# Which weights come first in a decode layer: w_1 and the MLP's features moved ahead of w_q

## The chip, the cores and the metric

The kernel runs on one core of one Trainium2 chip. The metric is device time in microseconds (us), the median of several executions. A profile of one execution says where the time of that execution lies. The core has five engines that run side by side and wait for each other by semaphores: TensorE (PE, matrix products), VectorE (DVE), ScalarE (ACT), GpSimd (POOL) and SyncE (SP). Here SP does nothing but issue transfers, one after the other, so a transfer that has to wait holds back all the transfers behind it. ACT issues a few small transfers on a queue of its own.

## What is computed

One token goes through two branches, which a gate mixes:

```python
g = sigmoid((x * gate_w).sum(-1))                       # one number
q = x @ wq                                              # 576 -> 32 heads of 128
k, v = the last 4096 of 32768 positions of the caches   # 16 heads, each for two query heads
a = softmax(q k^T / sqrt(128)) v  @ wo                  # attention branch
b = gelu(x @ w1 + b1) @ w2 + b2                         # MLP branch, 576 -> 4608 -> 576
out = g * a + (1 - g) * b
```

Everything is bfloat16 in memory. With one token each weight and each cached key is used once, so the work is to read 53.62 MB: four key tiles and four value tiles of 4096 KB each, w_q and w_o with 4608 KB each, w_1 with 5184 KB and w_2 with as much.

## The kernel before

**Tiles and buffers.** The 16 key/value heads are done four at a time, t = 0 to 3. Key tile k_t[t] and value tile v_t[t] hold four heads of the window. All eight, and w_2's two halves after them, go through one pool of three buffers (kv_pool, L80); a new tile is loaded when the buffer's last reader is done. w_q, w_1 and w_o share one buffer (w_pool, L81). The order of the program on each engine is that of the text (manual_schedule, L90).

**Order of the transfers on SP.** w_q, k_0, k_1, b_1, the gate's weights, k_2, v_0, k_3, w_1, v_1, v_2, v_3, w_o, w_2 in five pieces, and the output. By the three buffers, v_0 takes k_0's place, k_3 takes k_1's, v_1 takes k_2's, v_2 takes v_0's, v_3 takes k_3's, and w_2's halves take v_1's and v_2's. Each of these is issued when the last reader of the old tile is done: for keys the DVE transposes, for values the matmuls of `values`. w_1 needs the buffer of w_q, and w_o that of w_1, which `w1_mul` reads last. Besides, the transfers take their completion semaphores in turn from a set of eight, so that the ninth shares one with the first and waits until that one has landed. In this program the first is w_q's, and the ninth is the first piece of the gate's weights (L151).

**Start.** x comes as one row (L137), is copied to an order by partitions (L171, ACT), spread over the partitions by nine matmuls with a one-element operand (L377) and masked by four DVE instructions into x2 (L387). Then 36 matmuls make q (L392), it is turned and written with zeros between into qz, the operand of the scores (L404 to L428).

**Attention.** Key tile t has four quarters, h = 4t to 4t+3. DVE transposes each (`transposes(h)`, L243) into one of four buffers kT, and eight matmuls of 512 columns make its scores (`scores(h)`, L265). For h below 12 a loop pass is scores(h), one step of the softmax of the tile before, transposes(h+4); for the last four it is transposes(h), scores(h), one step. `softmax(t)` is four steps: row_max (DVE, L284 and L289), turn_max (a PE transpose, L295, then DVE L296 and L299), spread (PE L306, DVE L307, the exponential on ACT L310) and turn (DVE, L316). `values(t)` is 32 matmuls (L335), and `heads_out(t)` takes their result (L353 to L367). `norm` makes the divisors (L530 to L542).

**Gate and MLP.** `gate_rows` (L510) stands after the second key tile's transposes, `gate` (L517 to L522) after the third tile's scores. `w1_mul`, 72 matmuls with w_1 (L449), stands behind the last scores; `gelu` (L468 to L497), which makes the features gt, stands behind `norm` and before `values(1)`.

**End.** The partial sums `part` take w_o's product for one half of the rows, then w_2's first half, then the rest of w_o (L664). They are copied (L672, L673) and added to y_ps, which takes b_2 times 1 - g first (L652, eight small matmuls, listed under L647) and the second half of w_2 row by row as its pieces land (L675 to L688). y goes out by L694.

Of the kernel before, what the change touches and what calls it, by code (L numbers as in the profile page):

```python
# [8 lines left out]
FP32 = mybir.dt.float32  # L9
# [7 lines left out]
def kernel(  # L17
# [15 lines left out]
    nc = tc.nc  # L33
# [78 lines left out]
    def load_k(m):  # L112
        return load_kv(A_k_cache, m, "k_t")

    def load_v(m):
        return load_kv(A_v_cache, m, "v_t")
# [3 lines left out]
    def load_flat(src, name):  # L120
        t = w_pool.tile([P, WMAX], BF16, name=name, tag="w")
        nc.sync.dma_start(out=t[:, 0 : src.shape[1]], in_=src)
        return t
# [7 lines left out]
    nc.gpsimd.memset(b2_r[:], 0.0)  # L131
    b2_f = const.tile([1, D], FP32, name="b2_f")

    for h in (slice(0, D // 2), slice(D // 2, D)):
        nc.scalar.dma_start(out=b2_r[:, h], in_=B_b2.rearrange("(o n) -> o n", o=1)[:, h])

    nc.scalar.dma_start(out=x_row[:], in_=A_x.rearrange("a b n -> (a b) n"))  # L137

    wq_t = load_flat(wq_flat, "wq_t")
    k_tiles[0] = load_k(0)  # L140

    k_tiles[1] = load_k(1)
    b1_r = const.tile([P, 2, FB], BF16, name="b1_r")
    nc.gpsimd.memset(b1_r[:], 0.0)
    for o in range(2):
        nc.sync.dma_start(
            out=b1_r[o : o + 32 * (NQ - 1) + 1 : 32],
            in_=B_b1.rearrange("(o t k n) -> o t k n", o=2, t=NQ, k=2)[o],
        )
    for h in (slice(0, D // 2), slice(D // 2, D)):  # L150
        nc.sync.dma_start(out=gw_row[:, h], in_=gate_w.rearrange("(o n) -> o n", o=1)[:, h])  # L151
    k_tiles[2] = load_k(2)


    ident = const.tile([P, P], BF16, name="ident")
    make_identity(nc, ident[:])
# [10 lines left out]
        out=row_f[:], in_=ident_f[:, 0 : 32 * (NQ - 1) + 1 : 32], axis=AX.X, op=ALU.add  # L167
    )

    x_d = small.tile([1, P, NM], BF16, name="x_d", tag="ms")  # L170
    nc.scalar.copy(  # L171
        out=x_d[:].rearrange("o (k e) m -> o k e m", e=2),
        in_=x_row[:].rearrange("o (k e m) -> o k e m", e=1, m=NM).to_broadcast(
            [1, P // 2, 2, NM]
        ),
    )
    nc.scalar.copy(out=b2_f[:], in_=b2_r[:])
    one = const.tile([1, 1], BF16, name="one")
    nc.gpsimd.memset(one[:], 1.0)
    par = const.tile([P, 2], FP32, name="par")  # L180
    for o in range(2):
        nc.vector.tensor_reduce(
# [57 lines left out]
    def transposes(h):  # L240
        kT[h] = kT_pool.tile([P, NCH * ND], FP32, name="kT", tag="kT")
        lo = (h % UT) * NCH * Dh
        nc.vector.transpose(  # L243
            out=kT[h][:],
            in_=k_tiles[h // UT][:].rearrange("p c d -> p (c d)")[:, lo : lo + NCH * Dh].bitcast(
                FP32
            ),
        )
# [124 lines left out]


    x_ps = ps_m.tile([P, NM], FP32, name="x_ps", tag="m")
    for m in range(NM):
        nc.tensor.matmul(  # L377
            x_ps[:, m : m + 1], lhsT=x_d[0:1, :, m], rhs=one[:], start=True, stop=True
        )
    ev, od = par[:, 0:1], par[:, 1:2]  # L380
    for dst, src, s in (
        (x2[:, 0::2, 0], x_ps[:, 0:5], ev),
# [2 lines left out]
        (x2[:, 1::2, 1], x_ps[:, 0:4], ev),  # L385
    ):
        nc.vector.tensor_scalar(out=dst, in0=src, scalar1=s, scalar2=None, op0=ALU.mult)  # L387

    q_ps = ps_a.tile([P, 2, 512], FP32, name="q_ps", tag="a")
    for b in range(NM * NQ):  # L390
        m, t = b // NQ, b % NQ
        nc.tensor.matmul(  # L392
            q_ps[32 * t : 32 * (t + 1), 0, 0:QC],
            lhsT=x2[:, m, :],
            rhs=wq_t[:, b * QC : (b + 1) * QC],
            start=(m == 0),
            stop=(m == NM - 1),
        )
    NI = QC // Dh
    qT = q_ps[:, 1, 0 : NI * NBP * 2 * NT].rearrange("p (i b n) -> p i b n", i=NI, b=NBP)  # L400
    q_r = small.tile([P, NI, NBP, NA, PI], BF16, name="q_r", tag="big")
    for i in range(NI):
        copy = nc.scalar.copy if i % 2 else nc.vector.tensor_copy
        copy(  # L404
            out=q_r[:, i].rearrange("p (b o) a u -> p b o a u", b=2)[:, :, :, 0, :],
            in_=q_ps[:, 0, i * Dh : (i + 1) * Dh].rearrange("p (b u o) -> p b o u", b=2, o=2),
        )
    for i in range(NI):
        copy = nc.scalar.copy if i % 2 else nc.vector.tensor_copy
        copy(  # L410
            out=q_r[:, i, :, 1:NA, :],
            in_=q_r[:, i, :, 0:1, :].to_broadcast([P, NBP, NA - 1, PI]),
        )
    for i in range(NI):
        for bp in range(NBP):
            nc.tensor.matmul(
                qT[:, i, bp, :],
                lhsT=q_r[:, i, bp].rearrange("p a u -> p (a u)"),
                rhs=sel[:].rearrange("p l b -> p (l b)"),
                start=True,  # L420
                stop=True,
            )


    for a in range(NA):
        rows = slice(PI * a, PI * (a + 1))
        lo = QX + PI * a
        nc.vector.tensor_copy(  # L428
            out=qz[rows, lo : lo + NR * QW].rearrange("p (b t w) -> p b t w", b=NBP, w=QW)[
                :, :, :, 0:R  # L430
            ].rearrange("p b t (l i) -> p b t l i", l=2),
            in_=qT[rows].rearrange("p i b (l t) -> p b t l i", l=2),
        )


    for h in range(UT):
        transposes(h)
    v_tiles[0] = load_v(0)

    U = F // 2  # L440
    h_box = []
# [66 lines left out]
    def gate_rows():  # L508
        junk = small.tile([1, D], BF16, name="junk", tag="big")
        nc.vector.tensor_tensor_reduce(  # L510
            out=junk[:], in0=x_row[:], in1=gw_row[:], scale=1.0, scalar=0.0,
            op0=ALU.mult, op1=ALU.add, accum_out=s0[:],
        )

    def gate():
        g_ps = ps_m.tile([P, 1], FP32, name="g_ps", tag="m")
        nc.tensor.matmul(g_ps[:], lhsT=ones_ff[0:1, :], rhs=s0[:], start=True, stop=True)  # L517
        ge = const.tile([P, 1], FP32, name="ge")
        nc.scalar.activation(out=ge[:], in_=g_ps[:], func=ACT.Exp, scale=-1.0)
        nc.vector.tensor_scalar(out=ge[:], in0=ge[:], scalar1=1.0, scalar2=None, op0=ALU.add)  # L520
        nc.vector.reciprocal(out=g_t[:], in_=ge[:])
        nc.vector.tensor_scalar(  # L522
            out=omg[:], in0=g_t[:], scalar1=-1.0, scalar2=1.0, op0=ALU.mult, op1=ALU.add
        )
# [28 lines left out]

    for h in range(UT):
        scores(h)
        transposes(h + UT)
    k_tiles[3] = load_k(3)
    w1_t = load_flat(w1_flat, "w1_t")  # L560
    chain = softmax(0)
    for h in range(UT, 2 * UT):
        scores(h)
# [1 line left out]
        transposes(h + UT)  # L565
    v_tiles[1] = load_v(1)
    chain = softmax(1)
    gate_rows()
    for h in range(2 * UT, 3 * UT):
        scores(h)  # L570
        chain.pop(0)()
        if h == 3 * UT - 2:
            values(0)
            v_tiles[2] = load_v(2)
    gate()
    chain = softmax(2)
    for h in range(3 * UT, 4 * UT):
        transposes(h)
        scores(h)
        chain.pop(0)()  # L580
    v_tiles[3] = load_v(3)
    w1_mul(w1_t)
    wo_t = w_pool.tile([P, WMAX], BF16, name="wo_t", tag="w")
    nc.sync.dma_start(out=wo_t[:, 0 : OJ * D], in_=wo_view[:, 0, :])
    row_max, turn_max, spread, turn = softmax(3)
    take, turn_out = heads_out(0)
    take_h, turn_h, act = gelu()
    row_max()
    turn_max()
    spread()  # L590
# [1 line left out]
    turn()  # L592
    turn_out()
    norm()
    take_h()
    turn_h()
    act()
    sums_start()
    values(1)
    take, turn_out = heads_out(1)  # L600
# [44 lines left out]
    def row_matmul(col, row, start, stop):  # L645
        for t, q in enumerate(parts):
            nc.tensor.matmul(  # L647
                y_ps[32 * t : 32 * t + 1, 0 : q.stop - q.start], lhsT=col, rhs=row[:, q],
                start=start, stop=stop,
            )  # L650

    row_matmul(omg[0:1, :], b2_f, True, False)  # L652

    part = part_box[0]
    late = [[(ow[:, i, 0:1], wo_t, i) for i in range(j, j + NQ)] for j in range(0, OJ, NQ)]
    blocks, late = late[: OJ // (2 * NQ)], late[OJ // (2 * NQ) :]
# [1 line left out]
        blocks.append([(gt[:, i, 0:1], w2_t[0], i) for i in range(j, min(j + NQ, RJ))])  # L658
    blocks += late
    last = {t: max(n for n, four in enumerate(blocks) if t < len(four)) for t in range(NQ)}  # L660
    for n, four in enumerate(blocks):
        for k in range(2):
            for t, (col, w, i) in enumerate(four):
                nc.tensor.matmul(  # L664
                    part[32 * t : 32 * t + 1, k, 0:DB],
                    lhsT=col,
                    rhs=w[:, i * D + k * DB : i * D + (k + 1) * DB],
                    start=(n == 0),
                    stop=(n == last[t]),
                )  # L670
    part_s = [const.tile([P, DB], FP32, name=f"part_{k}") for k in range(2)]
# [2 lines left out]

    for j in range(RJ):  # L675
        row_matmul(
            gt[:, j, NG - 1 : NG], w2_t[NG - 1][:, j * D : (j + 1) * D], False, j == RJ - 1
        )
        if j == JA - 1:
            for t, q in enumerate(parts):  # L680
                for k in range(2):
                    lo, hi = max(q.start, k * DB), min(q.stop, (k + 1) * DB)
                    if lo < hi:
                        nc.tensor.matmul(
                            y_ps[32 * t : 32 * t + 1, lo - q.start : hi - q.start],
                            lhsT=row_f[:], rhs=part_s[k][:, lo - k * DB : hi - k * DB],
                            start=False, stop=False,
                        )  # L688
# [36 lines left out]
```

## Time and profile before

| | |
|---|---|
| median of 3 executions | 133.68 us (133.24 to 133.75) |
| the profiled execution, its own time | 133.42 us |
| its span, first to last instruction | 131.6 us |
| mean granted clock of TensorE | 0.78 |
| busy: PE, DVE, ACT, POOL | 72.6, 73.5, 10.7, 3.9 us |
| DMA: bytes, share of 16 engines in the SP queue's packets | 53.70 MB, 95.2% |
| chain that ended last: DMA, DVE, PE | 40%, 35%, 17% of the span |

The span is 1.82 us shorter than the execution's own time. In the fences below, a line of the timeline has the start in us, the busy us, the engine, the source line, the operation and its count; in brackets stand the idle time ahead of it and what ended it. A line of the waits has who waited for whom, the sum in us, how often, and the longest. A line of the chain that ended last has the start, the us and what it was. Lines of the stretches (windows) give the stretch and its length, then the busy us of PE, weight loads, DVE, ACT and POOL, and as the last three numbers PE's granted clock, the DMA engines' busy share and GB/s.

### The profile page before, as it was taken

The numbers are of one execution on the slowest core, as the hardware profiler recorded it, in microseconds if no ns is written. First come the engines' busy times: TensorE is split into PE (matmuls) and PEld (weight loads), VectorE is DVE, ScalarE is ACT, GpSimd is POOL, SyncE is SP. The second block draws the span as 40 slices with busy tenths as digits, with TensorE's granted clock in tenths as the row PEclk, the third lists the DMA queues.
The fourth block names the chain that finished last, engine by engine and source line by source line (L and its number), as shares of the span: only waits on it lengthen the run. The fifth ranks groups of instructions, "written<-read, shape, count | busy, mean of one in ns | idle before, by whom it ended". The sixth has DMA issues, their size and how long they took to land.

```text
span 131.6 us, 1446 instructions
## 1 busy us (share of the span) xinstructions
PE 72.6 (55%) x602; PEld 31.4 (24%) x602; DVE 73.5 (56%) x113; ACT 10.7 (8%) x20; POOL 3.9 (3%) x11
## 2 busy tenths in 40 slices
PE   0000293099892299919919665398275655460781
PEld 0000232034330134303313212135130321130451
DVE  2900103999799999981379434647778347300011
ACT  2100504000000003000300000300300000000011
POOL 8300000000000000000000000000000000000000
PEclk9999999658999757986985559559955599655589
DMA  6898999999999899899999999999998989899960
GB/s 179 370 527 359 478 408 398 468 448 390 440 463 428 378 478 458 378 431 515 403 403 403 486 383 448 468 408 398 478 448 373 483 370 527 363 416 425 413 226 0
DMA packets 2337, 53.70 MB, mean 408 GB/s; under 512 B 270, under 2 KB 540, under 8 KB 668
## 3 DMA queue, kind: packets, MB, share of 16 engines
q1 hardware_dynamic: 2326, 53.62, 95.2%
q8 instruction: 4, 0.07, 0.2%
q14 instruction: 1, 0.01, 0.0%
q10 hardware_dynamic: 6, 0.00, 0.0%
HBM read 53.62 MB, written 0.00 MB: 407 GB/s over the span
## 4 chain that ended last, share of the span: by engine, by line
DMA 40%; DVE 35%; PE 17%; issue 4%; SPq 1%; ACT 0%; DVEq 0%
DMA k_t<-in_A_k_cache_dram 24%; DVE kT L243 19%; DMA w_t<-in_B_w_dram 16%; PE s_ps L265 11%; PE acc L335 4%; DVE ms L284 4%; DVE mx L289 3%; DVE a_s L357 2%; DVE hT L474 1%; DVE ez L316 1%; PE mb L306 1%; PE mT L295 1%; DVE h_r L468 1%; DVE m L296 1%; DVE m_all L299 0%
## 5 line engine op out<-in xcount | busy, mean ns | idle before, releaser
L265 PE MATMUL s_ps<-kT,qz 128*128 128x512 bf16 x128 | 40.6, 479 | 14.0 <-DVE kT L243 14.0
L243 DVE STREAM_TRANSPOSE kT<-k_t 128x2048 f32<-128x2048 f32 x16 | 36.1, 2285 | 1.0 <-DMA k_t<-in_A_k_cache_dram 0.9
L265 PEld LDWEIGHTS <-qz 128*128 128x128 bf16 x128 | 14.5, 115 | 36.5 <-issue 27.1
L335 PE MATMUL acc<-v_t,ez 128*32 128x512 bf16 x128 | 11.0, 488 | 0.0
L310 ACT ACTIVATE pr<-ms,nb 128x1024 bf16<-128x1024 f32 x4 | 4.6, 1148 | 64.7 <-DVE nb L307 64.7
L377 PE MATMUL x_ps<-one,x_d 1*128 1x1 bf16 x9 | 0.7, 195 | 14.8 <-ACT x_d L171 14.8
L672 DVE COPY part<-part 128x288 f32<-128x288 f32 x1 | 0.5, 457 | 12.8 <-PE part L664 12.8
L284 DVE TENSOR_TENSOR ms<-s_ps,off 128x1024 f32<-128x1024 f32 x4 | 4.8, 1210 | 2.3 <-PE s_ps L265 2.2
L365 PE MATMUL o_ps<-a_s,m_r 128*32 128x128 f32 x8 | 1.9, 319 | 7.7 <-DVE a_s L357 7.7
L295 PE MATMUL mT<-ident_f,mx 128*1 128x128 f32 x4 | 1.4, 358 | 8.3 <-DVE mx L289 8.3
L387 DVE TENSOR_SCALAR x<-x_ps,par 128x5 bf16<-128x5 f32 (+1 forms) x4 | 0.6, 229 | 9.2 <-PE x_ps L377 9.2
L316 DVE STREAM_TRANSPOSE ez<-pr 128x1024 bf16<-128x1024 bf16 x4 | 4.9, 1221 | 1.4 <-ACT pr L310 1.4
L664 PE MATMUL part<-wo_t,ow 128*1 128x288 bf16 x64 | 4.4, 427 | 1.7 <-DMA wo_t<-in_A_wo_dram 1.7
L335 PEld LDWEIGHTS <-ez 128*32 128x32 bf16 x128 | 4.2, 117 | 4.4 <-issue 2.9
L289 DVE TENSOR_REDUCE mx<-ms 128x1 f32<-128x1024 f32 x4 | 4.9, 1220 | 0.1
L664 PE MATMUL part<-w_t,gt 128*1 128x288 bf16 x36 | 2.6, 441 | 4.0 <-DMA w_t<-in_B_w_dram 4.0
L357 DVE SCALAR_TENSOR_TENSOR a_s<-acc,m_c,a_s 128x128 f32<-128x128 f32 x12 | 4.2, 351 | 0.4
L392 PE MATMUL q_ps<-wq_t,x 128*32 128x512 bf16 x36 | 4.0, 630 | 0.6 <-DVE x L387 0.6
L377 PEld LDWEIGHTS <-x_d 1*128 1x128 bf16 x9 | 0.6, 152 | 14.8 <-ACT x_d L171 14.8
L307 DVE TENSOR_SCALAR nb<-mb 128x1 f32<-128x1 f32 x4 | 0.6, 145 | 6.2 <-PE mb L306 6.2
L296 DVE TENSOR_REDUCE m<-mT 1x8 f32<-1x128 f32 x4 | 1.1, 268 | 4.7 <-PE mT L295 4.7
L158 DVE CAST ident_f<-ident 128x128 f32<-128x128 bf16 x1 | 1.9, 1900 | 2.3 <-POOL ident masks.py:199 2.3
(86 smaller groups left out, 49.5 us busy)
## 6 DMA issues: line engine op xcount, KB each, us to landing
k_t<-in_A_k_cache_dram SPq DMA_DIRECT2D x4, 4096.0 KB, 22.8
v_t<-in_A_v_cache_dram SPq DMA_DIRECT2D x4, 4096.0 KB
w_t<-in_B_w_dram SPq DMA_DIRECT2D x1, 5184.0 KB, 33.1
wq_t<-in_A_wq_dram SPq DMA_DIRECT2D x1, 4608.0 KB
wo_t<-in_A_wo_dram SPq DMA_DIRECT2D x1, 4608.0 KB
w_t<-in_B_w_dram SPq DMA_DIRECT2D x1, 2592.0 KB
w_t<-in_B_w_dram SPq DMA_DIRECT2D x1, 1872.0 KB
w_t<-in_B_w_dram SPq DMA_DIRECT2D x1, 576.0 KB, 21.4
```

The source lines that it names most:

```text
L243: nc.vector.transpose(out=kT[h][:], in_=k_tiles[h // UT][:].rearrange("p c d -> p (c d)")[:, lo : lo + NCH * Dh].bitcast(FP32),)
L265: nc.tensor.matmul(s_tiles[t][:, k].rearrange("p c i e -> p c (i e)"), lhsT=qz[:, r * QW + lo : r * QW + lo + P], rhs=kT_v[:, k * NCB : (k ...
L284: nc.vector.tensor_tensor(out=ms[:], in0=s_v, in1=off[:].rearrange("p (o e) -> p o e", o=1).to_broadcast([P, NCH * 8, HT]), op=ALU.add,)
L289: nc.vector.tensor_reduce(out=mx[:], in_=ms[:].rearrange("p x e -> p (x e)"), axis=AX.X, op=ALU.max)
L295: nc.tensor.transpose(out=mT[:], in_=mx[:], identity=ident_f[:])
L296: nc.vector.tensor_reduce(out=m8[:], in_=mT[:].rearrange("o (x r) -> o r x", r=R), axis=AX.X, op=ALU.max)
L310: nc.scalar.activation(out=pr[:].rearrange("p c j -> p (c j)"), in_=ms[:].rearrange("p x e -> p (x e)"), func=ACT.Exp, bias=nb[:, 0:1], sc ...
L316: nc.vector.transpose(out=ez[:, t].rearrange("p x c r -> p c x r"), in_=pr[:].rearrange("p c j -> p (c j)"),)
L335: nc.tensor.matmul(acc[t][32 * ct : 32 * ct + BC * R, :, :], lhsT=ez[:, t, x, c : c + BC, :].rearrange("p c r -> p (c r)"), rhs=v_tiles[t] ...
L357: nc.vector.scalar_tensor_tensor(out=a_s[:], in0=acc[t][:, c, :], scalar=m_c[:, c : c + 1], in1=a_s[:], op0=ALU.mult, op1=ALU.add,)
L392: nc.tensor.matmul(q_ps[32 * t : 32 * (t + 1), 0, 0:QC], lhsT=x2[:, m, :], rhs=wq_t[:, b * QC : (b + 1) * QC], start=(m == 0), stop=(m == ...
L664: nc.tensor.matmul(part[32 * t : 32 * t + 1, k, 0:DB], lhsT=col, rhs=w[:, i * D + k * DB : i * D + (k + 1) * DB], start=(n == 0), stop=(n ...
```

## The change

w_1 becomes SP's first transfer and k_0 the second. The making of q (L389 to L433) moves behind the first four transposes, its text unchanged. w_q follows k_0 and takes w_1's buffer, so it waits for `w1_mul`; k_1 and k_2 stand behind it. `w1_mul`, the gate and gelu are done right after x2, ahead of the first transposes and of q. x comes a second time as 64 rows of 9 (x9), and one matmul with a doubled identity (dup) spreads it. The small loads (b_2, x9, b_1, x, gate weights) are all issued by ACT. b_2's product goes into part's first quarter as its first two matmuls, ahead of w_o's, and no longer into y_ps.

As built, the changed kernel issues on SP: w_1; k_0; w_q; k_1; k_2; v_0; k_3; v_1; v_2; v_3; w_o; w_2 in five pieces; the output. The seven small transfers on ACT and w_1's take the eight completion semaphores; k_0 is the ninth, shares w_1's, and its issue waits until w_1 has landed. w_q waits for w_1's last reader (PE); w_o now waits only for w_q's landing and last reader, and all value tiles wait as before.

```diff
+    x9 = const.tile([P // 2, NM], BF16, name="x9")
     for h in (slice(0, D // 2), slice(D // 2, D)):
         nc.scalar.dma_start(out=b2_r[:, h], ...)
...
-    wq_t = load_flat(wq_flat, "wq_t")
-    k_tiles[0] = load_k(0)
-    k_tiles[1] = load_k(1)
...
+    nc.scalar.dma_start(out=x9[:], in_=A_x.rearrange("a b (i m) -> (a b i) m", m=NM))
     for o in range(2):
-        nc.sync.dma_start(
+        nc.scalar.dma_start(
             out=b1_r[o : o + 32 * (NQ - 1) + 1 : 32], ...
+    nc.scalar.dma_start(out=x_row[:], ...)
+    nc.scalar.dma_start(out=gw_row[:], ...)
+    w1_t = load_flat(w1_flat, "w1_t")
+    k_tiles[0] = load_k(0)
...
-    for m in range(NM):
-        nc.tensor.matmul(
-            x_ps[:, m : m + 1], lhsT=x_d[0:1, :, m], rhs=one[:], start=True, stop=True
-        )
+    nc.tensor.matmul(x_ps[:], lhsT=dup[:], rhs=x9[:], start=True, stop=True)
...
+    w1_mul(w1_t)
+    wq_t = load_flat(wq_flat, "wq_t")
+    k_tiles[1] = load_k(1)
+    k_tiles[2] = load_k(2)
+    gate_rows()
+    gate()
+    for f in gelu():
+        f()
+    for h in range(UT):
+        transposes(h)
+    v_tiles[0] = load_v(0)
+    q_ps = ps_a.tile([P, 2, 512], FP32, name="q_ps", tag="a")
...
     for h in range(UT):
         scores(h)
         transposes(h + UT)
     k_tiles[3] = load_k(3)
-    w1_t = load_flat(w1_flat, "w1_t")
...
-    gate_rows()
...
-    gate()
...
-    w1_mul(w1_t)
...
-    take_h()
-    turn_h()
-    act()
...
-    row_matmul(omg[0:1, :], b2_f, True, False)
...
+    for k in range(2):
+        nc.tensor.matmul(
+            part[0:1, k, 0:DB], lhsT=omg[0:1, :], rhs=b2_f[:, k * DB : (k + 1) * DB],
+            start=True, stop=False,
+        )
```

More of the change, by code (lines that the diff above doesn't have):

```diff
@@ L132 @@
     b2_f = const.tile([1, D], FP32, name="b2_f")
+    x9 = const.tile([P // 2, NM], BF16, name="x9")
+    b1_r = const.tile([P, 2, FB], BF16, name="b1_r")
+    nc.gpsimd.memset(b1_r[:], 0.0)
     for h in (slice(0, D // 2), slice(D // 2, D)):
         nc.scalar.dma_start(out=b2_r[:, h], in_=B_b2.rearrange("(o n) -> o n", o=1)[:, h])
-    nc.scalar.dma_start(out=x_row[:], in_=A_x.rearrange("a b n -> (a b) n"))
-    wq_t = load_flat(wq_flat, "wq_t")
-    k_tiles[0] = load_k(0)
-    k_tiles[1] = load_k(1)
-    b1_r = const.tile([P, 2, FB], BF16, name="b1_r")
-    nc.gpsimd.memset(b1_r[:], 0.0)
+    nc.scalar.dma_start(out=x9[:], in_=A_x.rearrange("a b (i m) -> (a b i) m", m=NM))
     for o in range(2):
-        nc.sync.dma_start(
+        nc.scalar.dma_start(
             out=b1_r[o : o + 32 * (NQ - 1) + 1 : 32],
@@ L149 @@
         )
-    for h in (slice(0, D // 2), slice(D // 2, D)):
-        nc.sync.dma_start(out=gw_row[:, h], in_=gate_w.rearrange("(o n) -> o n", o=1)[:, h])
-    k_tiles[2] = load_k(2)
+    nc.scalar.dma_start(out=x_row[:], in_=A_x.rearrange("a b n -> (a b) n"))
+    nc.scalar.dma_start(out=gw_row[:], in_=gate_w.rearrange("(o n) -> o n", o=1))
+    w1_t = load_flat(w1_flat, "w1_t")
+    k_tiles[0] = load_k(0)
     ident = const.tile([P, P], BF16, name="ident")
@@ L168 @@
     )
[L170 to L174, printed above, removed]
-        ),
-    )
-    nc.scalar.copy(out=b2_f[:], in_=b2_r[:])
-    one = const.tile([1, 1], BF16, name="one")
-    nc.gpsimd.memset(one[:], 1.0)
+    nc.scalar.copy(out=b2_f[:], in_=b2_r[:])
+    dup = const.tile([P // 2, P], BF16, name="dup")
+    nc.vector.tensor_copy(
+        out=dup[:].rearrange("k (i e) -> k i e", e=2),
+        in_=ident[0 : P // 2, 0 : P // 2].rearrange("k (i e) -> k i e", e=1).to_broadcast(
+            [P // 2, P // 2, 2]
+        ),
+    )
     par = const.tile([P, 2], FP32, name="par")
@@ L387 @@
         nc.vector.tensor_scalar(out=dst, in0=src, scalar1=s, scalar2=None, op0=ALU.mult)
[L389 to L438, printed above, removed]
     U = F // 2
@@ L550, in sums_start @@
         part_box.append(part)
+    w1_mul(w1_t)
[10 more added lines that the diff above has]
+    q_ps = ps_a.tile([P, 2, 512], FP32, name="q_ps", tag="a")
+    for b in range(NM * NQ):
+        m, t = b // NQ, b % NQ
+        nc.tensor.matmul(
+            q_ps[32 * t : 32 * (t + 1), 0, 0:QC],
+            lhsT=x2[:, m, :],
+            rhs=wq_t[:, b * QC : (b + 1) * QC],
+            start=(m == 0),
+            stop=(m == NM - 1),
+        )
+    NI = QC // Dh
+    qT = q_ps[:, 1, 0 : NI * NBP * 2 * NT].rearrange("p (i b n) -> p i b n", i=NI, b=NBP)
+    q_r = small.tile([P, NI, NBP, NA, PI], BF16, name="q_r", tag="big")
+    for i in range(NI):
+        copy = nc.scalar.copy if i % 2 else nc.vector.tensor_copy
+        copy(
+            out=q_r[:, i].rearrange("p (b o) a u -> p b o a u", b=2)[:, :, :, 0, :],
+            in_=q_ps[:, 0, i * Dh : (i + 1) * Dh].rearrange("p (b u o) -> p b o u", b=2, o=2),
+        )
+    for i in range(NI):
+        copy = nc.scalar.copy if i % 2 else nc.vector.tensor_copy
+        copy(
+            out=q_r[:, i, :, 1:NA, :],
+            in_=q_r[:, i, :, 0:1, :].to_broadcast([P, NBP, NA - 1, PI]),
+        )
+    for i in range(NI):
+        for bp in range(NBP):
+            nc.tensor.matmul(
+                qT[:, i, bp, :],
+                lhsT=q_r[:, i, bp].rearrange("p a u -> p (a u)"),
+                rhs=sel[:].rearrange("p l b -> p (l b)"),
+                start=True,
+                stop=True,
+            )
+    for a in range(NA):
+        rows = slice(PI * a, PI * (a + 1))
+        lo = QX + PI * a
+        nc.vector.tensor_copy(
+            out=qz[rows, lo : lo + NR * QW].rearrange("p (b t w) -> p b t w", b=NBP, w=QW)[
+                :, :, :, 0:R
+            ].rearrange("p b t (l i) -> p b t l i", l=2),
+            in_=qT[rows].rearrange("p i b (l t) -> p b t l i", l=2),
+        )
     for h in range(UT):
@@ L586 @@
     take, turn_out = heads_out(0)
-    take_h, turn_h, act = gelu()
     row_max()
@@ L660 @@
     last = {t: max(n for n, four in enumerate(blocks) if t < len(four)) for t in range(NQ)}
+    for k in range(2):
+        nc.tensor.matmul(
+            part[0:1, k, 0:DB], lhsT=omg[0:1, :], rhs=b2_f[:, k * DB : (k + 1) * DB],
+            start=True, stop=False,
+        )
     for n, four in enumerate(blocks):
@@ L667 @@
                     rhs=w[:, i * D + k * DB : i * D + (k + 1) * DB],
-                    start=(n == 0),
+                    start=(n == 0 and t > 0),
                     stop=(n == last[t]),
@@ L676 @@
         row_matmul(
-            gt[:, j, NG - 1 : NG], w2_t[NG - 1][:, j * D : (j + 1) * D], False, j == RJ - 1
+            gt[:, j, NG - 1 : NG], w2_t[NG - 1][:, j * D : (j + 1) * D], j == 0, j == RJ - 1
         )
```

## The prediction, made before the changed kernel ran

> **What bounds the kernel now.** I read the page's DMA row first, then the stretches, SP's waits, the chain that ended last and the timelines.
>
> The DMA row by slices, and the stretches between five landings that the trace shows (k_1, w_1, w_o, w_2's first half, the last piece):
>
> ```profile
> DMA  6898999999999899899999999999998989899960
> ```
> ```profile
> 1.00:33.60 32.60, 12.82 (x85) 5.68 (x86) 15.56 (x31) 4.36 (x7) 3.46 (x7) 0.90 0.99 419
> 33.60:76.40 42.80, 29.80 (x128) 11.40 (x126) 33.86 (x29) 2.65 (x5) 0.00 (x0) 0.78 1.00 429
> 76.40:116.40 40.00, 21.77 (x212) 9.49 (x211) 23.03 (x50) 2.71 (x5) 0.00 (x0) 0.71 1.00 432
> ```
>
> The DMA share is 0.99, 1.00, 1.00: the transfers never run dry, while no compute engine is full. The end, in the chain, is the last piece of w_2, from issue to landing; behind it come 131.6 - 128.36 = 3.24 us:
>
> ```profile
> 1.86 31.77 DMA k_t<-in_A_k_cache_dram
> ...
> 66.92 0.15 DVE omg L522
> 67.07 2.22 DVE kT L243
> ...
> 73.92 3.57 PE s_ps L265 x8
> ...
> 80.54 2.35 PE s_ps L265 x8
> ...
> 83.60 2.23 DVE kT L243
> 85.87 3.27 PE s_ps L265 x8
> ...
> 106.96 21.40 DMA w_t<-in_B_w_dram
> ```
>
> So a change gains or loses what it does to an unbroken stream, and the question is whether each transfer is still issued before the one ahead of it has landed. SP's waits and issues show how this holds now:
>
> ```profile
> SPq L104 <- DVE kT L243: 49.7, 4, 21.0
> SPq L151 <- DMA wq_t<-in_A_wq_dram: 10.4, 1, 10.4
> ```
> ```profile
> 0.73 0.40 SPq L122 DMA_DIRECT2D wq_t<-in_A_wq_dram  x1
> 1.19 1.44 SPq L104 DMA_DIRECT2D k_t<-in_A_k_cache_dram  x2
> 2.67 1.22 SPq L146 DMA_DIRECT2D b_r<-in_B_b_dram  x2
> 14.31 0.55 SPq L151 DMA_DIRECT2D gw_row<-in_gate_w_dram  x2
> ```
>
> SP waits long, but k_0 and k_1 were queued by 2.63. The wait for w_q's landing until 14.31, by the ninth transfer, is therefore covered by two key tiles.
>
> **Rates.** w_q: issue at 0.73, landing at 14.31, 13.58 us. From k_1's landing (33.63, end of the chain's first DMA) to w_o's (116.4, where PE's wait for it ends) lie k_2, v_0, k_3, w_1, v_1, v_2, v_3, w_o: 6 x 4.194 + 5.308 + 4.719 = 35.19 MB in 82.8 us, 0.425 MB/us. A key or value tile then takes 9.87 us, w_q 11.1. A transfer issued on an empty queue costs more: 13.58 - 11.1 = 2.5 us for w_q; the output's 1.1 KB, issued at 129.66, is in by the span's end, 1.94 at most. I take 2.2, between, and keep both.
>
> **The change part by part.**
>
> *First gap.* k_0's issue now waits for w_1's landing, with nothing queued behind w_1 on SP. w_1 has 0.59 MB more than w_q: landing at 14.31 + 0.59/0.425 = 15.7. k_0 lands at 15.7 + 2.2 + 9.87 = 27.8 instead of 25.6: **2.2 us** lost (1.9 to 2.5). Everything on SP queues behind it.
>
> The Trainium skill, page "DMA: Bandwidth & Descriptors", section on the anatomy of one DMA, gives a fixed cost near 2.0 us per transfer plus bytes over 436 GB/s, for the GpSimd path. By it the gap is 2.0, within the two rows.
>
> *w_q's issue.* It waits for w1_mul. x9 should land about with w_1: x_row, on the same queue, was used at 13.64, 0.67 before w_q landed. Then one matmul (nine took 0.69) and four DVE instructions (0.62): x2 by 17.0. The ACT copy of 1.15 falls out. 72 matmuls took 2.39 at 89.06; at the pace of the 36 after long idleness (L392, 4.03 us, 512 columns) they take 4.03 x 72 x 288/(36 x 512) = 4.5. PE is done by 21.5, and w_q, k_1, k_2 are issued while k_0 runs, 4 us before they must be (27.8 - 2.2). Cost 0. Landings: w_q 38.9, k_1 48.8, k_2 58.7, v_0 68.5, k_3 78.4, v_1 88.3, v_2 98.1.
>
> *The key chain.* k_0's transposes (27.8 to 36.7) come before w_q. From the start of q's matmuls to qz it took 16.17 to 23.89, 7.7: qz at 46.6, 20 us of delay against now. scores(0), 2.3 (9.21 for four), frees a kT buffer at 48.9, with k_1's landing; transposes 4 to 7, paced by 2.3 each, end at 58.1, against 42.65 now: **15.45 later**. From here the stages repeat those of before. k_2 (58.7) is there for its first transposes (45.08 + 15.45 = 60.5). The third tile's stage loses gate_rows (0.64) and the gate's wait (transposes(12) starts at 66.98, could at 65.11: 1.87). transposes(12) starts at 66.98 + 15.45 - 2.51 = 79.9, behind k_3's landing.
>
> *Second gap.* v_3 takes k_3's buffer, free when transposes(15) ends: 18.84 us after transposes(12) starts (66.98 to 85.82), so 98.8. v_2 lands at 98.1, so v_3 finds the queue empty and lands at 98.8 + 2.2 + 9.87 = 110.9 instead of 108.0: **2.9 us** lost. Now v_3 is issued at 85.8 with w_1, v_1 and v_2 at work ahead of it; the change has put w_1's 12.5 us ahead of this chain and left only k-tiles and values to cover it. Bounds: at full clock a score group takes 1.85, not 3.57 and 2.35 (the two on this path), and the stage 16.6; at half clock 20.1. The gap is then 0.7 to 4.1, and 0.4 to 4.4 with the issue's bounds.
>
> *Other edits.* gelu (97.16 to 101.20) and w1_mul (2.39) leave the end: the values' chain is only 1.25 shorter, since values(1) ends at 100.37 on PE anyway. ow is ready at 113.76 + 13.0 - 1.25 = 125.5. w_o lands near 122; its first 32 matmuls (2.1) end at 127.6, just before w_2's first half (122.53 + 5.1). So the shift of this chain stays hidden, with 0.1 to 0.6 us to spare; without the cover it costs what it is late. w_2's halves are issued after values(1) and values(2), near 113 and 119, before w_o lands. b_2: eight matmuls of 0.68 go; two fp32 matmuls of 288 columns, of which no row exists, come where PE waits for w_o or ow; 0 to 0.7, taken as 0. dup costs about what spread_o does (0.22) on idle DVE; ACT issues four more transfers (0.2 to 0.6 each) while it waits for b_2 anyway; one POOL memset (0.18) goes. All 0.
>
> **Sum.** 2.2 + 2.9 = 5.1 us. Profiled execution: 133.42 + 5.1 = **138.5 us**, span 136.7. The median shown is 0.26 above that execution, less than my rounding. Bounds: 1.9 + 0.4 gives 135.7, 2.5 + 4.4 gives 140.3.
>
> **Rivals.**
>
> *A: only the first gap costs.* v_3 is issued before v_2 lands, because the scores of the last tile run at full clock or q's matmuls do (4.03 would be 2.1). For it: the granted clock was 1.00 at 62 to 66 and 108 to 110.4. Against: 0.50, 0.50, 0.77, 0.58 in the four score groups at 69 to 89. Time 133.42 + 2.2, plus up to 0.7: 135.6 to 136.3. Chance 0.20.
>
> *B: the chain is slower than in this trace*: half clock through the whole stage and a further wait of PE or DVE in the second stage. Then gap two is 4.1 to 6, the time 140.3 to 142. For it: three of the four groups ran near 0.5. Chance 0.14.
>
> The Trainium skill, page "TensorE: Matmul & The Clock Gate", part on the HAM clock gate, has PE fall to half rate after an idle window of about 3.4 us. By that rule, waits of 3 us between groups might keep the clock up, which speaks for A; the rows (0.50 at 69 to 77.6, after waits of 3.05 and 1.01) do not follow it.
>
> *C: not slower.* The pauses let lagging DMA engines catch up. Place: the end of the stream, where 122.5 to 128.4 moved only 308 GB/s and the mean to 116.4 was 419 to 432. Price: 5.9 x (432 - 308)/432 = 1.7, and 32.6 x 13/432 = 1.0 at the start, 2.7 in all. It decides from the point where the second gap is below 0.5: then 133.42 + 2.2 - 2.7 = 132.9. With the second gap at 2.9 even this leaves 135.8. Chance 0.05: 0.02 faster, 0.03 same.
>
> *D: k_0 is not held by w_1* (a wait that ends early). Then all is 2.2 earlier, chain and stream alike, and the second gap remains: 136.3. The built order speaks against it. Chance 0.03.
>
> The forecast itself, both gaps at 137 to 140, has 0.58. The range that leaves out 2 in 10 reaches from A's lower side to B's first part: 135.5 to 140.8. The bound of 0.5% is about what a measurement of this kernel can tell from no change. Faster 0.02, same 0.03, slower 0.95.
>
> **What would show it.** First gap: k_0's issue near 15.7, a dip in the DMA row in slices 5 and 6, first transposes near 27.8. Second: SP's issue of v_3 near 98.8, waiting for transposes, and a dip just there, near slice 30. w_q issued near 21, with no dip behind k_0. If the DMA row has no dip, the theory is wrong; if ow comes after w_2's first half has landed, the values' chain sets the end and the time is above mine. If x9 landed only behind k_0, w_q would be issued near 33 and all would be some 8 us later still.

## The result, and the profile after

The changed kernel takes 142.72 us (median of six, 140.97 to 143.04) against 133.47 (133.15 to 133.75): slower, by a ratio of 1.0657 (95% interval 1.0591 to 1.0723). The forecast was 138.5, its range 135.5 to 140.8: the right way and the right two places, but 9.3 us instead of 5.1. The profiled execution took 143.04, its span is 141.2, 9.6 more than before. Here and below a median is over all executions, a ratio over those within 1.5% of the fastest of their kernel.

The DMA row of the page (mean busy share of the DMA engines in 40 slices, here of 3.53 us) answers to the one shown of before:

```profile
DMA  6999389979999999999999899994099999799950
GB/s 188 411 482 423 78 371 445 464 334 501 408 399 422 436 445 445 445 445 439 445 436 445 385 399 418 445 436 176 0 436 408 396 449 501 328 457 410 426 224 2
```

Before, no slice between the first and the end was below 8. Now there are two holes: a 3 in slice 5, and a 4 and a 0 in slices 28 and 29. The stretches between them (length, busy us of PE, weight loads, DVE, ACT, POOL, then PE's granted clock, DMA share, GB/s), first after, then the same bytes before:

```profile
1.00:14.30 13.30, 0.00 (x0) 0.10 (x1) 4.38 (x16) 1.95 (x2) 3.37 (x6) 1.00 0.99 399
14.30:17.00 2.70, 1.01 (x17) 0.71 (x20) 1.29 (x6) 0.00 (x0) 0.00 (x0) 1.00 0.02 4
17.00:96.10 79.10, 42.80 (x273) 18.23 (x265) 50.20 (x50) 4.24 (x10) 0.00 (x0) 0.80 1.00 430
96.10:102.50 6.40, 3.93 (x13) 1.55 (x12) 3.50 (x3) 1.24 (x2) 0.00 (x0) 0.77 0.04 15
102.50:138.00 35.50, 21.68 (x278) 9.56 (x277) 14.10 (x37) 1.64 (x3) 0.00 (x0) 0.67 0.95 402
```
```profile
1.00:14.50 13.50, 0.00 (x0) 0.00 (x0) 3.98 (x15) 2.15 (x2) 3.46 (x7) 1.00 0.95 389
14.50:93.50 79.00, 52.99 (x307) 22.00 (x307) 55.01 (x57) 6.28 (x14) 0.00 (x0) 0.78 1.00 432
93.50:128.40 34.90, 18.93 (x275) 9.01 (x276) 13.91 (x39) 1.69 (x4) 0.00 (x0) 0.66 0.96 409
```

The working stretches are as long as they were: 79.1 against 79.0 us, 35.5 against 34.9. The time went into the pauses, **2.7 and 6.4 us**, 9.1 of the 9.6. SP's timeline names both:

```profile
0.73 0.40 SPq L122 DMA_DIRECT2D w_t<-in_B_w_dram  x1
16.05 0.61 SPq L104 DMA_DIRECT2D k_t<-in_A_k_cache_dram  x1
20.51 0.34 SPq L122 DMA_DIRECT2D wq_t<-in_A_wq_dram  x1
...
72.62 29.14 SPq L104 DMA_DIRECT2D v_t<-in_A_v_cache_dram  x3
101.81 0.58 SPq L578 DMA_DIRECT2D wo_t<-in_A_wo_dram  x1
```

k_0 is issued at 16.05, when w_1 has landed. w_q is issued at 20.51 while k_0 runs, and costs nothing. The last of the three value tiles is issued at 101.2 (29.14 us are the stretch of all three) and w_o at 101.81 right behind it, although w_o's buffer had been free since q was made. DVE's timeline (start, busy us, in brackets the idle time ahead and what ended it) shows what v_3 waited for:

```profile
50.77 8.89 DVE L237 STREAM_TRANSPOSE kT<-k_t 128x2048 f32<-128x2048 f32 x4 [3.56 <-PE s_ps L259]
...
81.59 2.27 DVE L237 STREAM_TRANSPOSE kT<-k_t 128x2048 f32<-128x2048 f32 x1
...
98.90 2.30 DVE L237 STREAM_TRANSPOSE kT<-k_t 128x2048 f32<-128x2048 f32 x1
```

The second key tile's transposes wait for the first score group, transposes(12) starts at 81.59, transposes(15) ends at 101.2, and v_3 takes that tile's buffer. The chain that ended last still closes with the last piece of w_2 landing, at 137.97:

```profile
119.82 18.15 DMA w_t<-in_B_w_dram
138.01 0.54 PE y_ps L637 x15
```

### The profile page after: what moved, and what is told of

It is laid out like the page before. It is cut to its first block, busy times and chain, and to the rows that moved or that the text cites. A ratio compares the mean times of both kernels' runs of the same rounds, so it can differ in the third digit from the quotient of the medians.

```text
span 141.2 us, 1418 instructions
## 1 busy us (share of the span) xinstructions
PE 70.1 (50%) x590; PEld 30.5 (22%) x590; DVE 74.1 (52%) x114; ACT 9.6 (7%) x19; POOL 3.8 (3%) x10
## 4 chain that ended last, share of the span: by engine, by line
DMA 37%; DVE 32%; PE 24%; issue 2%; ACT 2%; DVEq 0%; SPq 0%; ACTq 0%
DMA w_t<-in_B_w_dram 24%; DVE kT L237 19%; DMA wq_t<-in_A_wq_dram 13%; PE s_ps L259 12%; PE acc L329 4%; DVE ms L278 3%; PE h_ps L389 3%; PE q_ps L511 3%; DVE mx L283 3%; DVE ez L310 3%; DVE a_s L351 2%; PE mb L300 1%; ACT pr L304 1%; DVE qz L547 1%; PE mT L289 1%
## 5 line engine op out<-in xcount | busy, mean ns | idle before, releaser
L259 PE MATMUL s_ps<-kT,qz 128*128 128x512 bf16 x128 | 36.4, 444 | 10.7 <-DVE kT L237 9.4
L259 PEld LDWEIGHTS <-qz 128*128 128x128 bf16 x128 | 13.5, 107 | 30.3 <-issue 18.6
L329 PE MATMUL acc<-v_t,ez 128*32 128x512 bf16 x128 | 9.8, 443 | 0.0
L511 PEld LDWEIGHTS <-x 128*32 128x32 bf16 x36 | 1.3, 139 | 20.7 <-DMA wq_t<-in_A_wq_dram 18.8
L389 PEld LDWEIGHTS <-x 128*32 128x32 bf16 x72 | 3.1, 145 | 12.0 <-issue 11.1
L389 PE MATMUL h_ps<-w_t,x 128*32 128x288 bf16 x72 | 4.3, 432 | 0.6 <-DMA w_t<-in_B_w_dram 0.6
L523 DVE CAST q_r<-q_ps 128x128 bf16<-128x128 f32 x2 | 0.6, 292 | 6.5 <-PE q_ps L511 6.2
## 6 DMA issues: line engine op xcount, KB each, us to landing
v_t<-in_A_v_cache_dram SPq DMA_DIRECT2D x4, 4096.0 KB, 12.3
```

The lines of the kernel that those rows point to most:

```text
L259: nc.tensor.matmul(s_tiles[t][:, k].rearrange("p c i e -> p c (i e)"), lhsT=qz[:, r * QW + lo : r * QW + lo + P], rhs=kT_v[:, k * NCB : (k ...
L329: nc.tensor.matmul(acc[t][32 * ct : 32 * ct + BC * R, :, :], lhsT=ez[:, t, x, c : c + BC, :].rearrange("p c r -> p (c r)"), rhs=v_tiles[t] ...
L389: nc.tensor.matmul(h_box[0][32 * t : 32 * (t + 1), k, 0:FB], lhsT=x2[:, m, :], rhs=w[:, off : off + FB], start=(m == 0), stop=(m == NM - 1),)
L511: nc.tensor.matmul(q_ps[32 * t : 32 * (t + 1), 0, 0:QC], lhsT=x2[:, m, :], rhs=wq_t[:, b * QC : (b + 1) * QC], start=(m == 0), stop=(m == ...
```

## The experiments

Each is compared with runs of the kernel before on the same chip, whose median is 133.22 us for k_0 freed, w_o ahead, both edits and the old order, and 133.36 for the other four. The theory: the loss is the two pauses, one from k_0's shared semaphore, one from a key chain that frees v_3's buffer too late, and what lies behind them is hidden. Its rivals: the late q sets the end by itself, whatever the transfers do; the values' chain takes over where a pause is closed; the small edits cost part of it.

**k_0 freed from w_1's semaphore.** b_2 in one piece instead of two, so that k_0 is the eighth transfer to take a semaphore and not the ninth.

```diff
-    for h in (slice(0, D // 2), slice(D // 2, D)):
-        nc.scalar.dma_start(out=b2_r[:, h], ...)
+    nc.scalar.dma_start(out=b2_r[:], in_=B_b2.rearrange("(o n) -> o n", o=1))
```

> The changed kernel with b_2 loaded in one piece: the small loads are then six, k_0 is the eighth transfer and shares no completion semaphore with w_1, so its issue (16.05 us in the changed kernel) should fall to near 1.2 us and the first pause of the transfers (14.5 to 17.0) should vanish. Two-pause theory: w_q's landing and all that hangs on it come 2.5 us earlier, the second pause (96.1 to 102.5) stays about 6.4 us long because v_3's issue and v_2's landing both move: about 140.3 us. Rival (late q alone sets the time, the pause at the start is caught up later): the key chain still starts at w_q's landing, and w_q must wait for w_1's product; if w_q then lands no earlier, about 142.7, no change.

Measured: 139.68 us (138.10 to 140.16), ratio 1.0496 (1.0462 to 1.0531). k_0 and the two pauses' places in this kernel:

```profile
1.20 0.62 SPq L104 DMA_DIRECT2D k_t<-in_A_k_cache_dram  x1
20.06 0.33 SPq L122 DMA_DIRECT2D wq_t<-in_A_wq_dram  x1
```
```profile
14.00:17.00 3.00, 0.86 (x15) 0.55 (x17) 0.63 (x4) 0.00 (x0) 0.00 (x0) 1.00 0.82 352
...
92.00:93.00 1.00, 1.00 (x3) 0.15 (x1) 0.00 (x0) 0.00 (x0) 0.00 (x0) 0.50 1.21 524
93.00:94.00 1.00, 0.72 (x3) 0.60 (x3) 0.24 (x2) 0.00 (x0) 0.00 (x0) 0.50 0.23 98
...
97.00:98.00 1.00, 1.00 (x4) 0.43 (x3) 0.27 (x1) 0.00 (x0) 0.00 (x0) 0.50 1.53 393
```

The first pause is gone (352 GB/s where there were 4) and the kernel gains 3.0 us; the second stays. In this execution, the fastest of the four, it is some 4.4 us instead of 6.4: v_2's bulk had passed at 93.0, and v_3's first bytes moved at 97.4. The last tile's stage was 1.9 us shorter (17.7 for 19.6), above all because its second score group ran at full clock, 1.90 us for 3.51. The late-q rival, no gain, falls.

**w_o ahead of v_3.**

```diff
-    v_tiles[3] = load_v(3)
     wo_t = w_pool.tile([P, WMAX], BF16, name="wo_t", tag="w")
     nc.sync.dma_start(out=wo_t[:, 0 : OJ * D], in_=wo_view[:, 0, :])
+    v_tiles[3] = load_v(3)
```

> The changed kernel with w_o issued ahead of v_3, so that w_o's 11 us cover the wait for k_3's buffer. The second pause should vanish, v_3 land near 117.5, before values(3) starts near 121. Theory that the transfers alone set the end: 6.4 us less, about 136.5. Rival, that behind the pause the values' chain is the next bound: ow is ready at 126.6 as now, two blocks of w_o (2.1 each) and one of w_2 (2.4) follow on TensorE, the partial sums end near 134.2 instead of 136.5 and the time is about 140.7. If w_o ahead of v_3 changes nothing (142.7), the pause was no cost at all.

Measured: 138.87 us (137.85 to 139.74), ratio 1.0421 (1.0362 to 1.048). 3.9 us of the 6.4 are won. TensorE's timeline at the end says where the rest is: the partial sums never wait for a transfer any more. They start when ow is ready and run through, so that the values' chain has become the bound, as the rival said, though 1.8 us sooner than it said:

```profile
125.78 1.83 PE L650 MATMUL part<-b_f,omg 1*1 1x288 f32 x4
127.54 2.09 PE L657 MATMUL part<-wo_t,ow 128*1 128x288 bf16 x32
129.42 2.37 PE L657 MATMUL part<-w_t,gt 128*1 128x288 bf16 x34
```

**Both edits.**

> Both edits together: b_2 in one piece, w_o ahead of v_3. Transfers alone: no pause is left, 142.9 - 2.5 - 6.4 = 134.0 us. Values' chain as the next bound: 2.5 us earlier than with w_o ahead alone, about 138.2. A value near 142.7 would show that neither pause matters.

Measured: 136.06 us (134.84 to 138.23), ratio 1.0182 (1.0118 to 1.0247), between the two forecasts. The DMA row has no hole left:

```profile
DMA  6999899898998999989999999989999899999810
```

Yet 2.8 us remain. The chain that ended last (start, us, what) no longer closes with a transfer:

```profile
122.49 0.22 PE ow_ps L614
122.71 1.60 PE part L649 x4
124.31 5.85 PE part L656 x97
```

These 1.60 and 5.85 us of matmuls stand between ow and y. Before, most of them were done while w_2 was still landing. Closing the pauses brought the transfers forward, and the values' chain, late with the keys, took their place. Not by much, though: 131 GB/s were still moving from 128 to 129, where before 14 were left, so the transfers end later than before as well, and how the 2.8 us divide is not shown.

**The end relieved.** Both edits, and b_2's matmuls put behind values(1), w_2's first half ahead of all of w_o.

```diff
     values(1)
+    for k in range(2):
+        nc.tensor.matmul(part[0:1, k, 0:DB], lhsT=omg[0:1, :], rhs=b2_f[...], ...)
...
-    blocks, late = late[: OJ // (2 * NQ)], late[OJ // (2 * NQ) :]
+    blocks = []
```

> The kernel with both pauses closed, and its end relieved: b_2's two matmuls stand behind values(1), and the partial sums take w_2's first half before all of w_o. Values' chain as the bound: TensorE's part of the end is shorter by 0.9 to 1.7 us, so about 135.0 instead of 136.1; with the spread between executions still above a microsecond. If the transfers were the bound there, nothing changes: 136.1.

Measured: 134.75 us (133.29 to 137.25, ten executions), ratio 1.0056 (1.0018 to 1.0094). The median is 1.4 us above before; the ratio leaves out the three slowest executions. That is as expected for the values' chain as the bound. The best executions reach before, the worst lose 4 us.

**The old order with the small edits.** The kernel before with x9 and its one matmul, the small loads on ACT, b_2 in one piece and in the partial sums.

```diff
-    nc.scalar.dma_start(out=x_row[:], ...)
+    nc.scalar.dma_start(out=x9[:], ...)
...
     wq_t = load_flat(wq_flat, "wq_t")
     k_tiles[0] = load_k(0)
     k_tiles[1] = load_k(1)
...
-    row_matmul(omg[0:1, :], b2_f, True, False)
```

> The kernel before with the small edits of the change alone: x9 and one matmul for x, the small loads on ACT (b_2 in one piece), b_2 into the partial sums; w_q stays the first transfer, w_1, gate and gelu stay where they were. Theory: these cost nothing beside the transfers, 133.4 us within 0.7. Rival, that the small loads, the fp32 matmuls of b_2 (1.94 us in the changed kernel) or x9 carry part of the 9.3 us: 135 or more.

Measured: 133.39 us (133.28 to 133.47, ten executions), ratio 1.0012 (1.0002 to 1.0021). The small edits cost some 0.2 us. With b_2 in one piece this run lacks the one small load that made k_0 the ninth transfer, so it says nothing about the first pause. The kernel with k_0 freed differs from this one in the order alone: 139.68 against 133.39, so the order by itself costs 6.3 us.

**Half of the score matmuls**, in the changed kernel.

```diff
-        for bp in range(NBP):
+        for bp in range(NBP // 2):
```

> The changed kernel with only half of the score matmuls (64 instead of 128; half of the products of queries and keys is left out), transfers and their order unchanged. If the pause ahead of v_3 is TensorE's pace in the key chain, transposes(15) ends 5 to 7 us earlier than 101.2 (the first group 1.7, the second tile's last 1.6, two groups of the last tile 3.4), v_3 is issued near 95, the pause shrinks from 6.4 to below 1 us and the time is about 137; the first pause stays. Rival, that the pause comes of something else that v_3 waits for: about 142.7.

Measured: 138.41 us (137.95 to 138.69), ratio 1.0361 (1.0314 to 1.0408). transposes(15) ends at 96.6, 4.6 us earlier, and the pause shrinks to 1.2 us, while the first one stays:

```profile
14.00:17.00 3.00, 0.89 (x17) 0.58 (x20) 1.24 (x6) 0.00 (x0) 0.00 (x0) 1.00 0.02 4
96.00:97.20 1.20, 0.59 (x2) 0.25 (x2) 1.20 (x2) 0.00 (x0) 0.00 (x0) 0.50 0.20 82
```

So TensorE's pace in the key chain does set v_3's issue. The last tile's stage took 16.6 us for 19.6. The gain was 4.3 us where 5.7 was expected, mainly because the first group, 1.7 us shorter by the forecast, brought the second key tile's transposes forward by only 0.4. They now waited for k_1 to land:

```profile
50.38 8.89 DVE L237 STREAM_TRANSPOSE kT<-k_t 128x2048 f32<-128x2048 f32 x4 [3.41 <-DMA k_t<-in_A_k_cache_dram]
```

The four matmuls of a group took 1.87 us, as long as eight at full clock (1.90), since the granted clock was 0.50 in each:

```profile
86.85 1.86 PE L259 MATMUL s_ps<-kT,qz 128*128 128x512 bf16 x4 [3.55 <-DVE kT L237]
91.76 1.87 PE L259 MATMUL s_ps<-kT,qz 128*128 128x512 bf16 x4 [2.84 <-DVE kT L237]
96.61 1.87 PE L259 MATMUL s_ps<-kT,qz 128*128 128x512 bf16 x4 [2.47 <-DVE kT L237]
```

**q early, w_1 still first.** Both pauses closed, and w_q as the second transfer, into a key buffer and a transpose buffer; k_0 and k_1 follow, k_2 takes w_q's place. k_0's transposes stand behind the making of q.

```diff
     w1_t = load_flat(w1_flat, "w1_t")
+    wq_a = kv_pool.tile([P, NH], BF16, name="wq_a", tag="kv")
+    wq_f = kT_pool.tile([P, NCH * ND], FP32, name="wq_f", tag="kT")
...
+    nc.sync.dma_start(out=wq_a[:], in_=wq_flat[:, 0:NH])
+    nc.sync.dma_start(out=wq_b, in_=wq_flat[:, NH:])
     k_tiles[0] = load_k(0)
+    k_tiles[1] = load_k(1)
```

> The kernel with both pauses closed, and w_q as the second transfer, into buffers of its own (a key buffer and a transpose buffer that are free then), so that q is ready near 34 us instead of 44; w_1 stays first. Theory that w_1's 5.3 MB ahead of all keys delay the key chain: k_1 then lands near 46 as before, transposes(4) start there instead of at 47.6, the whole chain gains 1.6 us and the time is 134.5. Rival, that q behind the first keys is what delays the chain: it gains most of 10 us, the transfers alone are the bound and the time is 133.5 or below, with transposes(12) starting near 70.

Measured: 136.53 us (134.83 to 137.01), ratio 1.0147 (1.0073 to 1.0222), the same as without it within the spread. qz was done at 34.8 instead of 44.0, and yet:

```profile
33.56 1.19 DVE L547 CAST qz<-q_ps 32x128 bf16<-32x128 f32 x4 [1.20 <-PE q_ps L535]
37.74 8.89 DVE L243 STREAM_TRANSPOSE kT<-k_t 128x2048 f32<-128x2048 f32 x4 [3.00 <-DMA k_t<-in_A_k_cache_dram]
47.51 8.89 DVE L243 STREAM_TRANSPOSE kT<-k_t 128x2048 f32<-128x2048 f32 x4 [0.88 <-DMA k_t<-in_A_k_cache_dram]
```

Now both tiles' transposes wait for their keys; transposes(4) start at 47.5, where they started at 47.6 with q late, and transposes(12) at 78.35 against 78.59. So q, 9 us earlier, does not bring the chain forward: the second key tile's landing holds it at the same place. That tile landed at 33.63 before, and ahead of it only w_1's 5.3 MB have been added, some 12.5 us at the rate of the forecast. My 1.6 us were not there: k_1 landed at 47.5 and not at 46. The ninth transfer is now w_q's second piece, and its issue waited for w_1's landing as k_0's did, until 15.79, but with w_q's first piece queued behind w_1 no pause came of it.

**Both together**: q early and the end relieved.

> As with w_q second, and the relieved end too. With the chain 1.6 us earlier and its end 1 us shorter the transfers should be the bound again: 133.5 to 134.0, with a spread between executions as small as before's. Below 133.2 would mean that the new order beats the kernel before; nothing in the transfers says so.

Measured: 134.18 us (133.56 to 134.77, ten executions), ratio 1.006 (1.0031 to 1.0088). The best form of the new order that was tried, and still not better than before. The forecast of 133.5 to 134.0 was a little too low. In its profiled execution (134.68 us) the partial sums start with the landing of w_2's first half, at 122.23, and TensorE runs through from there to y at 130.2: its part of the end is still the last.

```profile
111.02 11.22 DMA w_t<-in_B_w_dram
122.28 5.93 PE part L661 x97
```

Before, that half was there no earlier (122.53), but ow was ready at 113.76, and w_o's first 32 matmuls were done ahead of it. Here ow is ready at 121.9 and all of them stand behind.

## Why the prediction was right in kind and wrong in size

*What bounds the kernel*: right. The transfers ran unbroken before, at the same rate outside the pauses after, and the small edits alone cost 0.2 us (the old order with them).

*First gap*: right in cause, and a little above its bounds: 2.7 us for 2.2 (1.9 to 2.5). w_1 landed at 16.03 instead of 15.7, k_0 at 28.5 instead of 27.8; freeing k_0 gave back 3.0 us. Semaphore sharing, one small transfer too many, was the whole cause.

*w_q's issue*: right, at 20.51 for "near 21", no hole behind k_0, w_q landed at 39.45 for 38.9. x9 was used at 15.36.

*The key chain*: the step that failed. v_3 was issued at 101.2 for 98.8, 2.4 us late. It began with the second key tile's transposes, at 50.77 for 48.9. "scores(0), 2.3 (9.21 for four)" took the mean of four groups, but the first took 3.48 us now. In the trace of before the weight loads of the first ten of these 32 matmuls come 0.43 us apart and the other 22 twice as fast:

```profile
47.26 3.48 PE s_ps L259 x8
```
```profile
26.36 0.10 PEld L265 LDWEIGHTS <-qz 128*128 128x128 bf16 x1 [2.31 <-issue]
26.74 0.14 PEld L265 LDWEIGHTS <-qz 128*128 128x128 bf16 x1 [0.28 <-issue]
...
30.15 0.14 PEld L265 LDWEIGHTS <-qz 128*128 128x128 bf16 x1 [0.28 <-issue]
30.58 4.70 PEld L265 LDWEIGHTS <-qz 128*128 128x128 bf16 x22 [0.28 <-issue]
```

Before, nothing waited for the first group alone, so its own length never showed. But k_1's landing, which I put at 48.8, was late too: with half of the scores the transposes waited for it until 50.38. So two things ended there almost together, and either alone would have held the chain past 50; the group's own share is at most some 0.4 us. Why k_1 took some 11 us behind w_q instead of 9.87 is not shown. transposes 4 to 7 ended at 59.66, for 58.1, and the last tile's stage took 19.6 us for 18.84: its two score groups on the chain took 3.51 and 3.35 us, for 3.57 and 2.35 before.

*Second gap*: right in place and cause (half the scores nearly closed it; w_o ahead filled it), wrong in size: 6.4 us of idle DMA for 2.9. 2.4 is v_3's later issue. The other 1.1 is how I reckoned the pause. I measured it from v_2's landing, 98.1, and the bulk of v_2 had passed by 96.1, 2.0 us sooner: a landing trails the transfers' bulk, and engines without work idle meanwhile (66 GB/s from 96.5 to 98). And I let v_3 begin 2.2 us after its issue, where its first bytes moved after 1.3, 0.9 us sooner:

```profile
96.00:96.50 0.50, 0.50 (x3) 0.22 (x2) 0.00 (x0) 0.00 (x0) 0.00 (x0) 0.50 0.00 0
...
97.00:98.00 1.00, 1.00 (x4) 0.15 (x1) 0.00 (x0) 0.00 (x0) 0.00 (x0) 0.50 0.15 66
...
102.50:103.00 0.50, 0.50 (x2) 0.15 (x1) 0.00 (x0) 0.00 (x0) 0.00 (x0) 0.50 1.44 393
```

My own landings contradicted my sum: carried on from v_3's 110.9 with w_o's 11.1 and w_2's 12.5, they gave an end at 134.5, where the gaps added to the old end, 128.36, gave 133.5. The lower bound of 0.4 and the upper of 4.4 were so both too low. In all 4.5 us were missed: 0.5 in the first gap, 3.5 in the second, 0.5 in the stretches between.

*Two readings that were wrong*, though no term hangs on them: when v_3 was issued before, at 85.8, w_1 had landed already (76.4), so only the end of v_1 and v_2 lay ahead of it; and qz at 46.6 is 22.7 us later than before, not 20.

*Other edits*: mostly right. gelu's 4 us ahead of the end bought nothing. b_2's matmuls, "0 to 0.7", took 1.94 us. PE then waited 2.38 us for w_2's first half, so they cost nothing in the changed kernel; once the pauses were closed they stood in the chain that ended last, with 1.60 us.

*Rivals*: A held for no execution in full. The freed k_0's fastest execution shows its mechanism in part: one more score group at full clock, and the second pause is 2 us shorter. B came nearest, and in part for its reasons: DVE waited 3.56 us for the first score group, and the last tile's stage, at 19.6 us, came close to the 20.1 of half clock throughout. But PE's granted clock was not lower on the whole (0.80 in the long stretch against 0.78 before), and the gap was above B's 6. C fell: outside the pauses the rate did not rise (430 against 432 GB/s). D fell with k_0's issue at 16.05.

*The clock-gate page*: "TensorE: Matmul & The Clock Gate" of the Trainium skill, in its part on the HAM clock gate, has PE at half rate until it has been busy for a window. With half of the scores, PE's mean granted clock fell from 0.795 to 0.70 (0.70, 0.71 and 0.79 in the other executions), and the last three groups ran at 0.50 in the profiled one. That agrees with the page, though I took the rows of before to speak against its rule; no run separates less work in a group from the longer waits between groups.

What stays open: why the same kernel's executions differ by up to 4 us once TensorE is on the path (133.29 to 137.25 in the relieved one), at mean granted clocks of 0.782 to 0.859 that do not order them. One profile for each kernel does not show which groups ran slow in the other executions.

## What to carry to other kernels

In a kernel whose transfers never pause, an order of loads is worth what it does to the latest moment at which each buffer comes free: draw up for every transfer its issue against the end of the one ahead, and pay for each miss by the time from the bulk's end to the next first byte. Here bytes put ahead of a long dependent chain delayed the whole chain by about their transfer time, however early the chain's other input was, and what was hidden behind the last transfers may then become the end. A duration that is taken as the mean of a group must be looked up for the member that the new path waits for, and where two inputs arrive close together both must be priced.

## What the runs showed of the hardware beyond that

A transfer on an empty queue took 12.3 us from issue to landing for 4096 KB (v_3), where tiles on a busy queue follow each other by 9.7 (two tiles from w_q's landing at 14.31 to k_1's at 33.63); its first bytes moved 1.3 us after the issue, at 102.5. Small loads on ACT's queue did not have to wait for the large one on SP's, but gained unequally: b_2, issued at 1.33, had landed by 10.53, 5.5 us before w_1, while x9, issued at 2.13, came at 15.36, only 0.7 before it.
